# Twelve instead of six Strassen blocks in the first matrix, C11 begun by a bank-to-bank copy, score products as single blocks, sums added by transfers

## The chip, the cores and the metric

One core of a Trainium2 chip runs the whole program. The metric is the device time of one execution in microseconds, the median of the runs; lower is better. The engines are TensorE (PE; its weight loads are listed apart as PEld), VectorE (DVE), ScalarE (ACT), GpSimd (POOL) and SyncE (SP). POOL and SP issue nearly all transfers; each engine takes its instructions strictly in the order of its own program.

## The reference

Sparse attention is followed by a two-layer network, with batch 4, 8 heads, 768 positions and head size 64. A query sees the first 8 positions and the last 96, with a linear bias by distance.

```python
scores = scale * np.matmul(q, k.transpose(0, 1, 3, 2))
...
scores = np.where(keep, scores + bias, -1e9)
a = softmax(scores)
x = (a @ v) as 3072 tokens x 512
h = x @ w_in            # 512 x 2048, the first matrix
g = h - np.tanh(h)
out = g @ w_out         # 2048 x 512, the second matrix
```

## The kernel before

**Tiles.** The 3072 tokens are 24 units u of 128 queries, the four batches' first units ahead of all others. A unit has one or two blocks of keys (its own, o=0, and the one before it, o=1). For a unit the steps are: loads lq, lk, lv; transposes T (on PE with copies Te for the first seven units, by DMA on SP later); score products S (L396); the exponential E on ScalarE (L403); the mask M on VectorE; the product with v, AV (L427), whose 65th column is the sum of a row; its reciprocal R; the normalised x, N (L444); a transpose into xT (X and Xe on PE for eight units, Xe by DMA on SP later).

**First matrix.** The units are taken in groups: 0 and 1 alone, 2 to 11 in pairs (groups 2 to 6), and then fours (group 7 is units 12 to 15, 8 is 16 to 19, 9 is 20 to 23). A plain step m1 (L477) multiplies weights with xT into one PSUM bank; th takes tanh on ScalarE (L576) and g subtracts on VectorE (L590), into the tile gall. For groups of four, a block j of four 128-wide column blocks can be done by the Winograd form of Strassen's method instead: seven products d1 to d7 of half the size (L536, 28 matmuls of 256 columns where the plain way has 16 of 512). In before six blocks are done so (DUNITS): j = 1 to 3 of groups 8 and 9. Their sums of inputs are y (of x) and v (of weights). Copies e0, e1 and e2 keep the partial results of bank r; VectorE adds them back: q11 (L547), q21 and q22 (L550). tanh and g (L562, L568) then take 1024 columns at a time.

**Second matrix.** All twelve pairs of units are done in this form: p1 to p7 (L645, eight matmuls each), input sums n1 to n4 on VectorE (L630), weight sums w1 to w4 once, copies a0 to a2 out of bank r into the tile sn, and results c11, c21, c22 (an add on VectorE, L659) and c12 (a copy). Stores st go out from POOL or SP (L662). Where p6 adds onto bank r, it waits until a0 has read p1 there.

**Order.** No scheduler decides on the chip: the string ORDER lists every step in one sequence, each engine's program is the steps that fall to it in that order, and a suffix /a, /d, /p or /s picks ScalarE, VectorE, POOL or SP. HOMES gives each step its buffer or its PSUM banks (eight banks of 512 floats, which all these steps share). The score products of units 8 and up are written three blocks at a time, 24 matmuls in a row (the list runs, step S.n); those of units 0 to 7 are written unit by unit. So PE has 19 runs of score products.

## Time and profile before

| what | value |
|---|---|
| median of 3 runs | 201.99 us (201.69 to 202.01) |
| span of the profiled execution | 199.8 us |
| PE busy | 193.1 us, 97% of the span |
| VectorE busy | 178.6 us, 89% |
| ScalarE busy | 135.1 us, 68% |
| POOL busy | 75.3 us, 38% |
| chain that ended last, PE's share | 85% |

The profile gives the span from the first to the last instruction of one execution; its own run time is not given beside it, and the span lies 2.2 us under the runs' median. Matmuls are pipelined: a row's duration runs from issue to modelled end and overlaps with the next, so the price of a product on PE is the distance from its start to the start of the next. In a row of the timeline the columns are start, duration, engine, line, operation, written<-read, shape and count; idle time ahead of it stands in brackets with what ended it. A row of the groups gives, after the count, the busy time, the mean in ns of one, and idle time with what ended it.

### The profile page before, as it was taken

The page shows a single profiled execution, that of the slowest core. Times are in us where ns is not written, and L with a number is a line of the kernel's source. Part 1 is how long each engine was busy: PE and PEld are TensorE (multiplying, and loading weights), DVE is VectorE, ACT ScalarE, POOL GpSimd, SP SyncE. Part 2 cuts the span into 40 slices and gives each one's busy share as a digit, 9 for nine tenths or more (in the row PEclk, how much of TensorE's full clock was granted, in tenths as well). Part 3 has the DMA queues.
Part 4 walks back from the last instruction along what each step waited for, and adds up shares of the span by engine and source line. Part 5 has one row for each costly group of instructions (what it writes and reads, how often), then busy time and mean ns, then how long its engine had stood idle before and what let it go on. Part 6 is the DMA issues. An engine that isn't in the chain of part 4 may idle for free.

```text
span 199.8 us, 5524 instructions
## 1 busy us (share of the span) xinstructions
PE 193.1 (97%) x2219; PEld 157.8 (79%) x2219; DVE 178.6 (89%) x348; ACT 135.1 (68%) x234; POOL 75.3 (38%) x97
## 2 busy tenths in 40 slices
PE   8799999999999999999999999999999999999992
PEld 2469998888888988988898655688898687888892
DVE  6487599999999999999999898999999999999942
ACT  3698898726569559758947789578778777464220
POOL 8987576350694057069207904702000100001110
PEclk9999999999999999999999999999999999999999
DMA  5999999999999999989996998994733101001233
GB/s 148 211 180 185 198 163 207 201 156 141 193 167 196 178 153 135 133 188 171 137 158 146 140 173 192 154 155 85 55 108 121 66 0 54 3 0 52 107 132 131
DMA packets 103545, 27.36 MB, mean 137 GB/s; under 512 B 93920, under 2 KB 101472, under 8 KB 103520
## 3 DMA queue, kind: packets, MB, share of 16 engines
q0 software_dynamic: 74048, 16.78, 89.5%
q1 hardware_dynamic: 28928, 9.70, 27.6%
q10 hardware_dynamic: 544, 0.52, 1.0%
q8 instruction: 17, 0.28, 0.5%
q14 instruction: 8, 0.07, 0.1%
HBM read 27.26 MB, written 6.29 MB: 168 GB/s over the span
## 4 chain that ended last, share of the span: by engine, by line
PE 85%; DVE 7%; DMA 3%; ACT 2%; issue 1%; ACTq 0%; DVEq 0%
PE ps L645 36%; PE ps L477 27%; PE ps L536 9%; PE ps L396 5%; PE ps L427 5%; DMA f<-in_q_dram 3%; DVE gall L590 2%; DVE x L444 2%; DVE mem L407 1%; PE ps L455 1%; ACT mem L403 1%; PE ps L320 1%; ACT mem L274 1%; PE ps L365 1%; ACT th L576 1%
## 5 line engine op out<-in xcount | busy, mean ns | idle before, releaser
L477 PE MATMUL ps<-xT,w_in_bf 128*128 128x256 bf16 (+2 forms) x544 | 69.0, 279 | 0.0
L477 PEld LDWEIGHTS <-w_in_bf 128*128 128x128 bf16 x544 | 47.2, 98 | 12.4
L576 ACT ACTIVATE th<-ps 128x512 f32<-128x512 f32 (+1 forms) x74 | 41.8, 591 | 18.7 <-PE ps L477 13.6
L590 DVE TENSOR_TENSOR gall<-ps,th 128x512 bf16<-128x512 f32 (+1 forms) x74 | 47.4, 668 | 6.0 <-ACT th L576 5.6
L645 PEld LDWEIGHTS <-gall 128*128 128x128 bf16 x488 | 46.4, 98 | 7.0
L662 POOL DMA_DIRECT2D out_dram<-ot x14 | 8.1, 580 | 102.5 <-ACT ot L274 52.4
L403 ACT ACTIVATE mem<-ps 128x1024 bf16<-128x1024 f32 x44 | 43.3, 1024 | 4.3 <-PE ps L396 4.2
L645 PE MATMUL ps<-w_out_bf,gall 128*128 128x256 bf16 (+1 forms) x296 | 36.3, 270 | 0.0
L274 ACT COPY sn<-ps 128x256 f32<-128x256 f32 x32 | 12.0, 375 | 20.3 <-PE ps L645 16.3
L645 PE MATMUL ps<-f,ss 128*128 128x256 bf16 x192 | 24.9, 273 | 0.0
L645 PE MATMUL ps<-wc,gall 128*128 128x256 bf16 x192 | 24.9, 273 | 0.0
L342 POOL DMA_DIRECT2D vb<-in_v_dram x24 | 21.5, 900 | 2.2 <-issue 1.0
L645 PEld LDWEIGHTS <-ss 128*128 128x128 bf16 x192 | 18.3, 98 | 2.8
L342 POOL DMA_DIRECT2D mem<-in_k_dram x20 | 17.9, 899 | 4.8 <-DMA w_out_bf<-in_moe_w_out_dram 3.1
L342 POOL DMA_DIRECT2D mem<-in_q_dram x20 | 18.1, 904 | 3.8 <-DMA w_out_bf<-in_moe_w_out_dram 3.0
L412 DVE TENSOR_TENSOR mem<-mem,mk 128x2048 bf16<-128x2048 bf16 x16 | 19.2, 1215 | 0.0
L659 DVE TENSOR_TENSOR ot<-ps,sn 128x256 f32<-128x256 f32 x36 | 14.7, 415 | 3.6 <-ACT sn L274 2.5
L444 DVE TENSOR_TENSOR x<-ps,rden 128x512 bf16<-128x512 f32 x23 | 15.8, 687 | 0.5
L274 ACT COPY mem<-ps 128x512 f32<-128x512 f32 (+1 forms) x22 | 12.7, 585 | 5.1 <-PE ps L536 3.9
L427 PEld LDWEIGHTS <-mem 128*128 128x128 bf16 x352 | 13.4, 97 | 2.1 <-ACT mem L403 0.5
L427 PE MATMUL ps<-vb,mem 128*128 128x65 bf16 x352 | 14.7, 193 | 0.0
L396 PE MATMUL ps<-mem 64*128 64x128 bf16 x352 | 13.1, 217 | 0.0
(78 smaller groups left out, 220.7 us busy)
## 6 DMA issues: line engine op xcount, KB each, us to landing
out_dram<-ot POOLq DMA_DIRECT2D x14, 256.0 KB, 2.8
vb<-in_v_dram POOLq DMA_DIRECT2D x24, 128.0 KB, 6.2
mem<-in_q_dram POOLq DMA_DIRECT2D x22, 128.0 KB, 6.3
mem<-in_k_dram POOLq DMA_DIRECT2D x22, 128.0 KB, 6.1
out_dram<-ot SPq DMA_DIRECT2D x9, 256.0 KB, 2.0
w_out_bf<-in_moe_w_out_dram POOLq DMA_DIRECT2D x4, 512.0 KB, 10.7
w_in_bf<-in_moe_w_in_dram POOLq DMA_DIRECT2D x4, 256.0 KB, 7.6
w_in_bf<-in_moe_w_in_dram POOLq DMA_DIRECT2D x2, 512.0 KB, 11.0
```

Of the source, the lines that this page charges most:

```text
L274: nc.scalar.copy(out=out, in_=in_)
L342: eng(e).dma_start(out=dst, in_=rows_of(src, u).rearrange("h p d -> p h d"))
L396: nc.tensor.matmul(bank(("s", u, o), hh)[:, p * P : (p + 1) * P], buf(("qk", back[u] if o else u))[r, 1, p, :], buf(("qk", u))[r, 0, p, :] ...
L403: nc.scalar.activation(d, banks(("s", u, o), 0, 1), AF.Exp, bias=0.0, scale=scale)
L412: nc.vector.tensor_tensor(out=t, in0=t, in1=mk[:, 1:3], op=ALU.mult)
L427: nc.tensor.matmul(t[:, h // (H // 2), h % (H // 2), :], buf(("p", u, o))[:, slot(h), :], buf(("v", back[u] if o else u))[:, h, 0 : Dh + 1 ...
L444: nc.vector.tensor_tensor(out=buf(("x", u)).rearrange("q (a h) d -> q a h d", a=2), in0=t[:, :, :, 0:Dh], in1=rden.to_broadcast([P, 2, H / ...
L477: nc.tensor.matmul(t[:, (f - f0) * n : (f - f0 + 1) * n], w_in_bf[j][:, c, fo : fo + P], x[:, c, 0:n], start=(c == 0), stop=(c == CD - 1),)
L536: nc.tensor.matmul(t[:, r * 2 * P : (r + 1) * 2 * P], w(r)[:, c], x[:, c], start=first and r + c == 0, stop=c == 1, skip_group_check=not f ...
L576: nc.scalar.activation(h_view(buf(("th", g, f0)), g, m), h_view(bank(("h", g, f0)), g, m), AF.Tanh, bias=0.0, scale=1.0)
L590: nc.vector.tensor_tensor(out=o, in0=v(h), in1=v(th), op=ALU.subtract)
L645: nc.tensor.matmul(bank((holder, a))[:, c0:c1], s(f), t(f)[:, c0:c1], start=first and f == 0, stop=f == HF - 1, skip_group_check=not first,)
```

## The change

**More Strassen blocks.** DUNITS now holds j = 0 to 3 of groups 7, 8 and 9, twelve blocks. Of the plain steps of 512 columns none is left. The sums of the weights have a tile of their own (ws), and the shared buffers mem go from 23 to 20, xT from 4 to 3, ss from 5 to 3.

**C11 begun by a copy.** In both matrices, the copy of the first product (a0, e0) now goes from bank r to bank q, always on ScalarE, and the second product (p2, d2) adds onto it. The adds q11 are gone, and c11 is a plain copy, on ScalarE for eight pairs and on VectorE for four. p2 and d2 now wait for a0 and e0.

**Sums by transfer.** The signs of the weight sums are turned so that n3 and n4 are additions into gall; eleven of the 24 (n4 of pairs 8 to 16 and 20, n3 of pairs 10 to 14, 18 and 20) are issued from POOL as transfers that add onto their destination. gall is laid out unit by unit for that, and the products of a Strassen block write each bank in two pieces of 128 columns, 256 apart.

**Score products.** Each block of eight is a step of its own, S.u.o, and ORDER places them one by one. Neighbours on PE counted as one, there are 25 runs.

**Order.** ORDER and HOMES are new throughout. Stores: 15 on SP and 11 on POOL, against 12 and 14.

```diff
-m1.4.14 g.4.10 M.8 a1.4/a S.9 th.4.14 T.11 p5.4 g.4.14 E.9.1 V.7/d p2.4 a2.4/d E.10.0 M.9 T.12 m1.4.2 E.10.1 n4.4/d
...
+th.5.8 y1.7 m1.6.4 g.5.10 e0.7.0 lv.19 th.6.2 y2.7 c21.6 lk.22 d6.7.0 g.5.8 S.18.1 e1.7.0/a lv.18 v4.0 d2.7.0 th.6.4
...
+n2.22/d p3.18 n4.22/d p6.22 c12.18/a c21.16 st.18.0/s p4.18 a1.22/a n2.20/d p5.22 c21.18 n4.20/p st.19.0/s p6.20
...
-    NM, NV, NG, NSS, NSN = 23, 12, 5, 5, 4
+    QUADS = 12
+    NM, NV, NG, NSS, NSN, NXT = 20, 12, 5, 3, 4, 3
...
-    DUNITS = [(8, 1), (8, 2), (8, 3), (9, 1), (9, 2), (9, 3)]
+    DUNITS = [(g, j) for g in range(7, 10) for j in range(4)]
...
-    THREES = 8
...
-        else:
-            runs += [[(u, 0), (u, 1), (u + 1, 0)], [(u + 1, 1), (u + 2, 0), (u + 2, 1)]]
...
-    gall = pool.tile([P, NG, CF, 2 * P], BF16, name="gall")
+    gall = pool.tile([P, NG, 2, CF, P], BF16, name="gall")
...
-    def a_S(xs):
-        for u, o in xs:
-            for p in range(NP):
-                for hh in range(2):
-                    r = slice(hh * Dh, (hh + 1) * Dh)
-                    nc.tensor.matmul(
-                        bank(("s", u, o), hh)[:, p * P : (p + 1) * P], buf(("qk", back[u] if o else u))[r, 1, p, :],
-                        buf(("qk", u))[r, 0, p, :], start=u >= BIASED, stop=u >= BIASED or p == NP - 1,
-                    )
+    def a_S(u, o):
+        for p in range(NP):
+            for hh in range(2):
+                r = slice(hh * Dh, (hh + 1) * Dh)
+                nc.tensor.matmul(
+                    bank(("s", u, o), hh)[:, p * P : (p + 1) * P], buf(("qk", back[u] if o else u))[r, 1, p, :],
+                    buf(("qk", u))[r, 0, p, :], start=u >= BIASED and p == 0, stop=p == NP - 1,
+                )
 
...
     def d_keep(g, j, k):
-        return buf(("k0", g, j)) if k == 0 else mems(("k12", g, j), FP32)[:, (k - 1) * 4 * P : k * 4 * P]
+        return d_bank(g, j, "q") if k == 0 else mems(("k12", g, j), FP32)[:, (k - 1) * 4 * P : k * 4 * P]
...
-            2: ("q", lambda r: w_in_of(a + r, 2), x_block(g, 2, 1), True),
+            2: ("q", lambda r: w_in_of(a + r, 2), x_block(g, 2, 1), False),
...
-        t = d_bank(g, j, part)
+        t = d_bank(g, j, part).rearrange("q (t r n) -> q t r n", t=2, r=2)
...
-                    t[:, r * 2 * P : (r + 1) * 2 * P], w(r)[:, c], x[:, c], start=first and r + c == 0, stop=c == 1,
+                    t[:, :, r, :], w(r)[:, c], x[:, c], start=first and r + c == 0, stop=c == 1,
...
-        if k == 0:
-            q = d_bank(g, j, "q")
-            nc.vector.tensor_tensor(out=q, in0=q, in1=d_keep(g, j, 0), op=ALU.add)
-            return
...
-        o, x, y, op = {
-            1: (lambda: buf(("ss", a, 1)), lambda: a21, lambda: a22, ALU.add),
-            2: (lambda: buf(("ss", a, 2)), lambda: buf(("ss", a, 1)), lambda: a11, ALU.subtract),
-            3: (lambda: a21, lambda: a11, lambda: a21, ALU.subtract),
-            4: (lambda: a12, lambda: a12, lambda: buf(("ss", a, 2)), ALU.subtract),
-        }[k]
-        eng(e).tensor_tensor(out=o(), in0=x(), in1=y(), op=op)
+        (a11, a12), (a21, a22) = ((gall[:, i, t, 0:HF, :], gall[:, i, t, HF:CF, :]) for t in range(2))
+        one = lambda: buf(("ss", a, 1))
+        two = lambda: buf(("ss", a, 2))
+        o, x, y = {
+            1: lambda: (one(), a21, a22), 2: lambda: (two(), one(), a11),
+            3: lambda: (a21, a21, a11), 4: lambda: (a12, a12, two()),
+        }[k]()
+        if e is POOL:
+            nc.gpsimd.dma_start(out=o, in_=y, accum_op=ALU.add)
+        else:
+            eng(e).tensor_tensor(out=o, in0=x, in1=y, op=ALU.add)
...
-            2: ("q", lambda f: g_of(a, HF + f), w(1, 0), True),
+            2: ("q", lambda f: g_of(a, HF + f), w(1, 0), False),
...
     def keep(e, a, k):
-        copy(e, buf(("sn", a, k)), bank(("r", a))[:, 0:DH2])
+        copy(e, buf(("sn", a, k)) if k else bank(("q", a))[:, 0:DH2], bank(("r", a))[:, 0:DH2])
 
     def result(e, a, i, j, c0=0, c1=DH2):
         o = buf(("ot", a + i - 1))[:, (j - 1) * DH2 + c0 : (j - 1) * DH2 + c1]
-        if (i, j) == (1, 2):
-            copy(e, o, bank(("r", a))[:, c0:c1])
+        if i == 1:
+            copy(e, o, bank(("qr"[j - 1], a))[:, c0:c1])
             return
-        holder, k = {(1, 1): ("q", 0), (2, 1): ("z", 1), (2, 2): ("z", 2)}[i, j]
-        nc.vector.tensor_tensor(out=o, in0=bank((holder, a))[:, 0:DH2], in1=buf(("sn", a, k)), op=ALU.add)
+        nc.vector.tensor_tensor(out=o, in0=bank(("z", a))[:, 0:DH2], in1=buf(("sn", a, j)), op=ALU.subtract)
...
-            op((f"e{k}", g, j), None, lambda e, g=g, j=j, k=k: d_copy(e, g, j, k))
-        for w, k in (("q11", 0), ("q21", 1), ("q22", 2)):
+            op((f"e{k}", g, j), None if k else ACT, lambda e, g=g, j=j, k=k: d_copy(e, g, j, k))
+        for w, k in (("q21", 1), ("q22", 2)):
...
-            op((f"a{k}", a), None, lambda e, a=a, k=k: keep(e, a, k))
+            op((f"a{k}", a), None if k else ACT, lambda e, a=a, k=k: keep(e, a, k))
...
-            op((f"c{i}{j}", a), None if (i, j) == (1, 2) else DVE, lambda e, a=a, i=i, j=j: result(e, a, i, j))
+            op((f"c{i}{j}", a), None if i == 1 else DVE, lambda e, a=a, i=i, j=j: result(e, a, i, j))
```

The program of ScalarE in the last third, before: three copies of bank r (the last is e2 of block 1 of group 9), a0 of pair 16 into sn, tanh of a plain step, a copy e2, tanh of a Strassen block, a1.

```order
L274 COPY mem_81<-ps_61 128x512 x3
L274 COPY sn0_108<-ps_61 128x256
L576 ACTIVATE th_101<-ps_61 128x512
L274 COPY mem_81<-ps_61 128x512
L562 ACTIVATE th_101<-ps_61 128x1024
L274 COPY sn3_111<-ps_61 128x256
```

The same engine and place after: e0 of block 3 of group 9, e2 of block 1, a0 of pair 16, a tanh, c11 of pair 16 (ps is PSUM, mem, sn and ot are SBUF).

```order
L267 COPY ps_61<-ps_61 128x512
L267 COPY mem_81<-ps_61 128x512
L267 COPY ps_61<-ps_61 128x256
L551 ACTIVATE th_101<-ps_61 128x1024
L267 COPY ot2_113<-ps_61 128x256
```

The copies e0 and a0 now write PSUM, the plain tanh of 512 columns is gone, and c11 has come to this engine as a copy.

The program of POOL around the last loads, before: two stores, the loads of k 23, v 18 and v 20, a store, and v 22.

```order
L662 DMA out_0_dram<-ot1_114 128x512
L662 DMA out_0_dram<-ot3_116 128x512
L342 DMA mem_81<-in_k_dram 128x8x64
L342 DMA vb2_84<-in_v_dram 128x8x64
L342 DMA vb5_87<-in_v_dram 128x8x64
L662 DMA out_0_dram<-ot0_113 128x512
L342 DMA vb4_86<-in_v_dram 128x8x64
```

After: v 18, k 20, a store, the first transfer that adds (n4 of pair 8), then the loads of q 21, v 23 and v 20 and a store.

```order
L335 DMA vb6_88<-in_v_dram 128x8x64
L335 DMA mem_81<-in_k_dram 128x8x64
L657 DMA out_0_dram<-ot2_113 128x512
L624 DMA gall_102<-ss1_104 128x1024
L335 DMA mem_81<-in_q_dram 128x8x64
L335 DMA vb1_83<-in_v_dram 128x8x64
L335 DMA vb2_84<-in_v_dram 128x8x64
L657 DMA out_0_dram<-ot0_111 128x512
```

The transfer into gall stands among the loads: POOL waits there for n2 and p2 of pair 8, and the loads behind it wait along.

More of the change, by code (lines that the diff above doesn't have):

```diff
@@ L478, in m1 @@
                     t[:, (f - f0) * n : (f - f0 + 1) * n], w_in_bf[j][:, c, fo : fo + P], x[:, c, 0:n],
-                    start=(c == 0), stop=(c == CD - 1),
+                    start=f == f0 and c == 0, stop=(c == CD - 1),
+                    skip_group_check=f > f0,
                 )
@@ L494, in wsum @@
     def wsum(j, k):
[L495 removed]
+        return ws[:, j, k - 1]
     def xsum(g, k):
@@ L734 @@
             op(("Xe", u), SP, lambda e, u=u: a_DX(u))
-    for n, xs in enumerate(runs):
-        op(("S", n), PE, lambda e, xs=xs: a_S(xs))
+    for u in range(NU):
+        for o in blocks_of(u):
+            op(("S", u, o), PE, lambda e, u=u, o=o: a_S(u, o))
     for g, us in enumerate(groups):
```

242 lines of the change are left out of this document (119 added, 123 removed).

## Prediction

> **What bounds the kernel now.** I read the page first: busy time, slices, the chain that ended last.
>
> ```profile
> span 199.8 us, 5524 instructions
> PE 193.1 (97%) x2219; PEld 157.8 (79%) x2219; DVE 178.6 (89%) x348; ACT 135.1 (68%) x234; POOL 75.3 (38%) x97
> PE   8799999999999999999999999999999999999992
> DVE  6487599999999999999999898999999999999942
> PE 85%; DVE 7%; DMA 3%; ACT 2%; issue 1%; ACTq 0%; DVEq 0%
> ```
>
> TensorE is busy 97% of the span and carries 85% of the chain. A busy share alone does not prove a bound, so next come the waits of PE, then its busy time by stage.
>
> ```profile
> PE ps L361 <- ACT mem L274: 1.2, 1, 1.2
> PE ps L795 <- DVE vb L316: 1.0, 1, 1.0
> PE ps L455 <- DVE x L444: 0.9, 3, 0.4
> 58.00:130.00 72.00, 72.00 (x855) 57.31 (x854) 67.97 (x126) 53.20 (x96) 34.67 (x43) 1.00 1.61 161
> 130.00:180.00 50.00, 50.00 (x510) 41.32 (x508) 49.93 (x86) 37.21 (x62) 2.04 (x3) 1.00 0.36 64
> ```
>
> In these two windows (columns: PE, PEld, DVE, ACT, POOL, clock) PE is busy for every one of 122 us at a granted clock of 1.00. The first two waits belong to the start, which the change leaves as it is; the last, 0.9 us, is all that PE still loses to another engine. So the time after the start is the sum of PE's products, and the change is worth what it does to that sum, plus whatever new waits it makes. VectorE is the second limit: 49.93 of 50 us busy from 130 to 180, yet without holding PE up.
>
> **The products of the first matrix.** The timeline gives starts; the distance between starts is a product's price, since ends overlap.
>
> ```profile
> 118.84 3.62 PE L477 MATMUL ps<-xT,w_in_bf 128*128 128x512 bf16 x16
> 122.29 0.65 PE L427 MATMUL ps<-vb,mem 128*128 128x65 bf16 x16
> 143.57 1.04 PE L536 MATMUL ps<-mem 128*128 128x256 bf16 x8
> 144.45 1.04 PE L536 MATMUL ps<-xT,w_in_bf 128*128 128x256 bf16 x8
> 145.32 0.60 PE L536 MATMUL ps<-xT,mem 128*128 128x256 bf16 x4
> ```
>
> Sixteen 512-wide matmuls take 122.29 - 118.84 = 3.45 us. That is one block (four columns of blocks, 512 tokens) done plainly. Sixteen 256-wide ones take 145.32 - 143.57 = 1.75 us, 0.109 each, so a Strassen block of 28 costs 3.06. Saved: 0.39 us a block. Six more blocks (group 7's four, block 0 of groups 8 and 9): -2.3 us. Nothing hides this, PE being full.
>
> **The score products.** They contract over 64 rows; all around them contracts over 128.
>
> ```profile
> 51.27 1.04 PE L645 MATMUL ps<-w_out_bf,gall 128*128 128x256 bf16 x8
> 52.24 0.62 PE L396 MATMUL ps<-mem 64*128 64x128 bf16 x16
> 52.79 0.66 PE L427 MATMUL ps<-vb,mem 128*128 128x65 bf16 x16
> 61.58 1.04 PE L477 MATMUL ps<-xT,w_in_bf 128*128 128x256 bf16 x8
> 62.55 0.84 PE L396 MATMUL ps<-mem 64*128 64x128 bf16 x24
> 63.32 1.05 PE L645 MATMUL ps<-f,ss 128*128 128x256 bf16 x8
> 64.21 1.04 PE L645 MATMUL ps<-w_out_bf,gall 128*128 128x256 bf16 x8
> ```
>
> Sixteen score matmuls take 0.55 us from start to start, 24 take 0.77: 0.22 for a block of eight. The run of 24 should then be 0.66, and is 0.11 longer. The eight wide matmuls ahead of it should take 0.87 and take 62.55 - 61.58 = 0.97, 0.10 more; those behind it take 0.89. Each run of score products so costs about 0.23 us beyond its matmuls, whatever its length. In the table of before, 44 blocks stand in 19 runs; in that of after, counting neighbours on PE as one, in 25 (four single ones for the first batch rows as before, then pairs, two runs of three, and four lone blocks: S.16.1, S.18.1, S.19.0, S.21.0). Six more runs: +1.4 us. So the smaller pieces give back over half of what Strassen saves.
>
> **VectorE, ScalarE and the copies.** Rows of the groups:
>
> ```profile
> L590 DVE TENSOR_TENSOR gall<-ps,th 128x512 bf16<-128x512 f32 x70 | 45.8, 682 | 5.5 <-ACT th L576 5.2
> L568 DVE TENSOR_TENSOR gall<-ps,th 128x1024 bf16<-128x1024 f32 x6 | 7.3, 1219 | 0.0
> L550 DVE TENSOR_TENSOR mem<-ps,mem 128x512 f32<-128x512 f32 x12 | 8.2, 682 | 0.0
> L547 DVE TENSOR_TENSOR ps<-ps,mem 128x512 f32<-128x512 f32 x6 | 4.1, 687 | 0.0
> L659 DVE TENSOR_TENSOR ot<-ps,sn 128x256 f32<-128x256 f32 x36 | 14.7, 415 | 3.6 <-ACT sn L274 2.5 <-PE ps L645 0.8
> L630 DVE TENSOR_TENSOR gall<-gall 128x1024 bf16<-128x1024 bf16 x12 | 8.2, 681 | 0.0
> L509 DVE TENSOR_TENSOR mem<-w_in_bf 128x512 bf16<-128x512 bf16 x5 | 2.1, 413 | 0.0
> L576 ACT ACTIVATE th<-ps 128x512 f32<-128x512 f32 x70 | 40.2, 602 | 18.7 <-PE ps L477 13.6 <-DVE rden L433 1.9 <-DVE gall L590 1.3
> L562 ACT ACTIVATE th<-ps 128x1024 f32<-128x1024 f32 x6 | 6.2, 1037 | 0.3 <-PE ps L536 0.2
> L274 ACT COPY sn<-ps 128x256 f32<-128x256 f32 x32 | 12.0, 375 | 20.3 <-PE ps L645 16.3
> L274 ACT COPY mem<-ps 128x512 f32<-128x512 f32 x18 | 10.3, 585 | 4.1 <-PE ps L536 3.9
> ```
>
> VectorE loses six adds of line 547 (4.1), eleven sums of line 630 that become transfers (7.5), 24 narrow subtractions (16.4) and eight net of the 0.415 us ops on C11 (3.3): -31.3. It gains 12 wide subtractions (14.6), 12 adds of line 550 (8.2), eight sums of inputs (3.3) and about 2 us of copies: +28. Net -3 us, from 178.6 to about 175. ScalarE loses 24 narrow tanh (14.4) and gains 12 wide ones (12.4), 17 copies of 512 (9.9) and seven net copies of 256 (2.6): +10, to 145, 73% of the span. Neither becomes the bound by its sum, and PE's sum does not see them.
>
> The bank-to-bank copy is now ahead of a product: p2 adds onto what a0 wrote, d2 onto e0. For a block of the first matrix d6, which adds onto the bank that e0 reads, already waited for that copy, and after has d2 behind d6 or no nearer to e0. No row shows a copy into PSUM; the nearest are 375 and 585 ns into SBUF, which I take. Between p1 and p2 PE has at least 0.87 us of other products, so the term is zero if ScalarE is free, and the second rival if not.
>
> **The rest.** The eleven accumulating transfers are new; the first rival prices them, and I take zero. They stand on POOL, where n4.8 holds back loads of q 21 and v 23 and 20 until p2.8 has been; those keep 5.9 us and more of PE work ahead of their use. With 20 buffers instead of 23 the tightest load, v 10, keeps 6.0 us between its place and its product, where before the tightest kept 7.9. Stores move from POOL to SP (12 to 15 there), ahead of transposes whose shortest cover is 3.9 us.
>
> ```profile
> L662 POOL DMA_DIRECT2D out_dram<-ot x14: 542/582/645, 51.3 to 192.2; - x14
> DMA to landing us min/median/max: 1.7/2.3/5.8
> L342 POOL DMA_DIRECT2D vb<-in_v_dram x24: 876/895/962, 4.4 to 138.5; - x24
> DMA to landing us min/median/max: 3.6/6.2/13.7
> 195.60 0.61 PE L645 MATMUL ps<-w_out_bf,gall 128*128 128x128 bf16 x8
> 195.80 0.42 DVE L659 TENSOR_TENSOR ot<-ps,sn 128x256 f32<-128x256 f32 x1 [0.58 <-PE ps L645]
> 196.24 0.29 DVE L276 COPY ot<-ps 128x128 f32<-128x128 f32 x1
> ```
>
> Each pair of rows is an issue line and the landing times of its transfers. A load takes 0.9 to issue and 6.2 to land, so v 10 may be late by up to a microsecond; slack in the score blocks ahead of it makes me take zero here, with +1 in the range. At the end, the last copy ran at 196.24, behind a VectorE op that waited for p4 of the last pair. After, p4.22 comes earlier and the last quarter is copied by ScalarE directly behind its product: a copy of 128 instead of two ops, -0.1 us.
>
> **Sum.** -2.3 + 1.4 - 0.1 = -1.0 us against the profiled span: 199.8 becomes 198.8. The runs' median, 201.99, lies 2.2 over that span, and I carry the 2.2 along: 201.0. About 0.2% (0.4 us) is what a measurement of this kernel can tell from no change.
>
> **Rival 1, slower: the accumulating transfers come late.** Between its place in the table and the product that needs it, n4.20 has five products of 0.87 on PE (p6.20, p7.22, p5.20, p4.22, p7.20, then p3.20), 4.4 us; n4.12 has 4.9, n4.8 5.1, n4.14 5.2, the other seven 7.0 and more. A store of the same 256 KB takes 0.58 to issue and 1.7 to 5.8 to land: 2.9 us at the median, 6.4 at most. If the sum needs both operands read, twice the median landing gives 5.2: n4.20 is 0.8 late, n4.12 0.3, n4.8 0.1, and these 1.2 us use up the gain (202.2). At 5.8 the stalls are 1.4 + 0.9 + 0.7 + 0.6 = 3.6, so 204.6; at 6.4 they are 2.0 + 1.5 + 1.3 + 1.2 = 6.0, so 207.0. It decides from 5.1 us on. For it: no transfer in this trace adds. Against it: late in the run the queues are nearly empty (DMA share 0.36 from 130 to 180). The Trainium skill (DMA: Bandwidth & Descriptors, anatomy of one DMA) fits 2.0 us plus bytes over 436 GB/s to a transfer of this path, which would make 2.6 here and no stall at all. Chance 13%; its time 204.6.
>
> **Rival 2, no change: products wait behind the copies.** Where one ScalarE op stands between the product and its copy, the copy ends late if that op has only just begun: p1.10 (a 1.04 tanh and 0.375 against 0.88 of cover, 0.5), p1.4 (exp, 0.3), d1.7.0 (0.3), d1.8.2 (0.3), p1.0, p1.16, d1.7.3 (0.1 each). All at their worst make 1.7 us, 202.7; half, 201.9. For it: ScalarE rises to 73%. Against it: before has the same cover of 0.87 in front of p6 and d6, and no wait of PE for such a copy. Chance 20%.
>
> **Rival 3, much slower: scattered outputs.** The 336 products of Strassen blocks now write two pieces of 128 into their bank instead of 256 in a row. No row shows such an output. If one cost 10% more (11 ns), 336 would cost 3.7 us and make 204.7; 3 ns would use up the gain. The Trainium skill states that rule: any non-contiguous access pattern slows matmuls significantly (PSUM — Partial Sum Buffer, specifications); no run here shows it. The pieces are 512 bytes long, so I give it 3%.
>
> **Rival 4, faster still.** VectorE's 3 us less also take PE's 0.9 us of waits for x away: 200.1. Against it: those waits lie before 58 us, where the load of VectorE hardly falls. Chance 13%.
>
> **How the numbers follow.** My sum gets 48%, with 200.4 to 201.6 as its own range; the rivals 13, 20, 3 and 13; 3% are for what I don't see. The range 200.0 to 203.7 leaves out the larger part of rival 1, rival 3, the lower end of rival 4 and most of the rest, together 2 in 10. Faster: nearly all of my sum, rival 4 and a little of rival 2, 0.61. Same: the middle of rival 2, 0.14. Slower: rivals 1 and 3 and the rest, 0.25.
>
> **What would show it.** Right: no 512-wide first-matrix matmul left after group 6; 28 matmuls of a block still in 3.06 us; 25 runs of score products with 0.23 around each; PE's own waits still under 1 us after the start. Wrong: PE waits on the transfer into gall ahead of p7 or p3 near the end (rival 1), on ps copied by ScalarE ahead of p2 or d2 (rival 2), or distances over 0.109 between products of a block (rival 3).

## The result

The changed kernel is 1.6% slower: the ratio to the kernel before is 1.016 (95% interval 1.013 to 1.019), about 205.0 us against 201.8. The forecast was 201.0, and the range ended at 203.7. Some executions of a kernel take longer, here three of six (208.6 to 212.7 us, against 203.9 to 205.8); times and ratios leave them out, but the traces of y3, w2, q4 and a2 show one, so the lengths of their waits prove nothing alone. The profiled execution, the shortest of the six, took 203.88 us with a span of 202.1, 2.3 us over the span before. That the mean lies another 1.1 us higher, no trace of this kernel shows in detail; the control w0 below, which differs only in the buffers of activated pairs, has further waits behind 90 us.

The page of the changed kernel, the same lines as before:

```profile
span 202.1 us, 5665 instructions
PE 191.2 (95%) x2291; PEld 163.7 (81%) x2291; DVE 176.0 (87%) x335; ACT 144.3 (71%) x244; POOL 83.0 (41%) x105
PE   7699998999999986899999999999999999999992
PE 74%; DMA 15%; ACT 3%; SPq 2%; issue 1%; DVE 1%; POOL 1%; ACTq 0%; POOLq 0%; DVEq 0%
```

PE has 1.9 us less to do, and the span is longer. The chain that ended last now runs over transfers for 15% (3% before), and PE's slices (of 5 us each) fall to 8, 6 and 8 from 71 to 86 us. The same place in two windows, of the kernel before and then of the changed one (us, busy of PE, PEld, DVE, ACT, POOL, clock, DMA share, GB/s; the DMA share adds up several queues and so can exceed 1):

```profile
70.00:85.00 15.00, 15.00 (x206) 13.15 (x205) 14.26 (x28) 11.22 (x19) 6.71 (x8) 1.00 1.66 139
```

```profile
70.00:85.00 15.00, 11.91 (x181) 9.53 (x179) 12.25 (x26) 10.55 (x18) 7.87 (x9) 1.00 1.93 179
```

PE loses 3.1 us of busy time in these 15 us, while transfers move more (179 GB/s against 139). What it waits for there, from the timeline of the changed kernel:

```profile
73.14 0.66 PE L419 MATMUL ps<-vb,mem 128*128 128x65 bf16 x16 [0.23 <-DMA vb<-in_v_dram]
...
76.53 1.03 PE L641 MATMUL ps<-wc,gall 128*128 128x256 bf16 x8 [1.20 <-DVE ot L654]
...
78.45 0.40 PE L388 MATMUL ps<-mem 64*128 64x128 bf16 x8 [0.34 <-DVE x L436]
79.47 1.91 PE L469 MATMUL ps<-xT,w_in_bf 128*128 128x256 bf16 x16 [0.62 <-DMA xT<-x]
...
84.31 0.84 PE L388 MATMUL ps<-mem 64*128 64x128 bf16 x24 [0.70 <-DMA mem<-mem]
```

In turn: v of unit 10; the product p4.4, whose bank VectorE empties late (by c22.4); the x of unit 10, which VectorE works out behind c22.4; the transposed x of units 8 and 9; the transposed unit 13. By distances from start to start, with each matmul at its usual price, PE loses 4.3 us from 70 to 90 us against 0.45 before: about 0.4, 1.4, 0.5, 0.8 and 0.9 at these five places, and the rest around score products. Summed so over the whole run: matmuls -2.6, the first 70 us -0.3, 70 to 90 us +3.8, later (mostly the six more runs of score products) +1.3. That makes +2.2 of the 2.3 us measured.

The queues behind these waits, from the timelines of VectorE, POOL and SP in the changed kernel:

```profile
76.05 0.42 DVE L654 TENSOR_TENSOR ot<-ps,sn 128x256 f32<-128x256 f32 x1 [1.94 <-DMA out_dram<-ot]
...
56.62 0.89 POOL L335 DMA_DIRECT2D mem<-in_k_dram  x1 [10.31 <-DVE mem L399]
...
74.09 0.87 POOL L335 DMA_DIRECT2D vb<-in_v_dram  x1 [5.02 <-PE ps L419]
...
55.87 13.65 SPq L370 DMA_TRANSPOSE mem<-mem  x3
69.58 0.97 SPq L657 DMA_DIRECT2D out_dram<-ot  x1
...
76.54 1.47 SPq L370 DMA_TRANSPOSE mem<-mem  x1
```

POOL stands for 10.3 us with the load of k 15, whose buffer is still in use, and all later loads stand behind it; then ten go out 0.87 us apart. SP therefore gets the transposes of 12 and 15 only after 66 us, the store of rows 0 behind them at 69.6, and c22.4, which needs that store's buffer, waits until 76. So the 1.4 and 0.5 us at p4.4 and the x of unit 10 hang on a store that lands late. At 74 us POOL has stood for another 5.0 us, with the load of v 13. The last row is the transpose of unit 13. Transfers issued at 77 us land late (last column, us):

```profile
vb<-in_v_dram POOLq DMA_DIRECT2D x1, 128.0 KB, 7.8
mem<-mem SPq DMA_TRANSPOSE x1, 7.7
```

76.54 + 7.73 = 84.27, and the scores of unit 13 start at 84.31. In the kernel before, the same unit's transpose, issued at 68.56, took 4.8.

**Lead.** I matched each transfer by its place in its queue with the step on PE that reads it, and took its lead: from landing to first use. Times in us:

| unit | scores at, before | lead | scores at, after | lead |
|---|---|---|---|---|
| 12 | 73.6 | 4.2 | 73.7 | 2.6 |
| 13 | 78.2 | 4.9 | 84.3 | 0.05 |
| 14 | 89.5 | 2.9 | 77.5 | 0.6 |
| 15 | 89.9 | 4.2 | 78.5 | 3.3 |
| 17 | 106.7 | 2.6 | 95.7 | 0.05 |
| 18 | 107.1 | 3.8 | 97.9 | 4.4 |
| 19 | 112.6 | 2.6 | 112.8 | 0.05 |

The order needs units 14, 15, 17 and 18 from 9 to 12 us earlier, since group 7 as a Strassen group wants all of units 12 to 15 at once. That this is what brings 17 and 18, of group 8, forward as well was not looked into. For v, the shortest lead of units 8 to 23 was 2.3; now v 10 has 0.05 (11.3 before) and v 16 has 1.3.

### The profile page after: what moved, and what is told of

It is laid out like the page before. It is cut to its first block, busy times and chain, and to the rows that moved or that the text cites. A ratio compares the mean times of both kernels' runs of the same rounds, so it can differ in the third digit from the quotient of the medians.

```text
span 202.1 us, 5665 instructions
## 1 busy us (share of the span) xinstructions
PE 191.2 (95%) x2291; PEld 163.7 (81%) x2291; DVE 176.0 (87%) x335; ACT 144.3 (71%) x244; POOL 83.0 (41%) x105
## 4 chain that ended last, share of the span: by engine, by line
PE 74%; DMA 15%; ACT 3%; SPq 2%; issue 1%; DVE 1%; POOL 1%; ACTq 0%; POOLq 0%; DVEq 0%
PE ps L641 33%; PE ps L529 17%; PE ps L469 13%; DMA mem<-mem 7%; DMA mem<-in_q_dram 5%; PE ps L388 5%; PE ps L419 5%; DMA mem<-in_k_dram 3%; SPq L458 1%; ACT th L566 1%; POOL mem L332 1%; ACT mem L395 1%; DVE x L436 1%; ACT x L432 1%; PE ps L447 0%
## 5 line engine op out<-in xcount | busy, mean ns | idle before, releaser
L469 PE MATMUL ps<-xT,w_in_bf 128*128 128x256 bf16 (+1 forms) x448 | 46.7, 257 | 0.7 <-DMA xT<-x 0.6
L469 PEld LDWEIGHTS <-w_in_bf 128*128 128x128 bf16 x448 | 37.9, 98 | 4.7 <-issue 0.8
L581 DVE TENSOR_TENSOR gall<-ps,th 128x512 bf16<-128x512 f32 (+1 forms) x50 | 31.7, 662 | 3.8 <-ACT th L566 3.7
L566 ACT ACTIVATE th<-ps 128x512 f32<-128x512 f32 (+1 forms) x50 | 28.5, 589 | 8.2 <-PE ps L469 6.9
L335 POOL DMA_DIRECT2D mem<-in_k_dram x20 | 18.2, 911 | 12.5 <-DVE mem L399 10.3
L529 PE MATMUL ps<-mem,ws 128*128 128x256 bf16 x144 | 20.2, 273 | 0.0
L529 PEld LDWEIGHTS <-ws 128*128 128x128 bf16 x192 | 17.9, 98 | 2.4
L267 ACT COPY mem<-ps 128x512 f32<-128x512 f32 (+1 forms) x27 | 15.5, 586 | 5.2 <-PE ps L529 3.8
L624 POOL DMA_DIRECT2D gall<-gall x5 | 4.4, 878 | 32.6 <-DVE ss L626 32.6
L539 DVE TENSOR_TENSOR mem<-ps,mem 128x512 f32<-128x512 f32 x24 | 15.9, 682 | 0.8 <-PE ps L529 0.7
L267 ACT COPY ot<-ps 128x256 f32<-128x256 f32 (+1 forms) x20 | 7.2, 366 | 12.5 <-PE ps L641 12.4
```

The lines of the kernel that those rows point to most:

```text
L267: nc.scalar.copy(out=out, in_=in_)
L335: eng(e).dma_start(out=dst, in_=rows_of(src, u).rearrange("h p d -> p h d"))
L469: nc.tensor.matmul(t[:, (f - f0) * n : (f - f0 + 1) * n], w_in_bf[j][:, c, fo : fo + P], x[:, c, 0:n], start=f == f0 and c == 0, stop=(c = ...
L529: nc.tensor.matmul(t[:, :, r, :], w(r)[:, c], x[:, c], start=first and r + c == 0, stop=c == 1, skip_group_check=not first or r > 0,)
L539: nc.vector.tensor_tensor(out=a, in0=d_bank(g, j, "z"), in1=a, op=ALU.add)
L566: nc.scalar.activation(h_view(buf(("th", g, f0)), g, m), h_view(bank(("h", g, f0)), g, m), AF.Tanh, bias=0.0, scale=1.0)
```

## The experiments

Theories: A, the place of a transfer in SP's queue; B, want of buffers; C, the sums by transfer (in the run y4 it means the order on PE); D, transfers in flight slow each other; E, lead; F, engines other than the transfers. Moves in ORDER are shown as the words that moved.

**First set: A, B and C.** Two stores ahead of the transposes; a buffer of its own for k and q 15; both; and all n3, n4 back on VectorE.

```diff
 # x1_stores_early
-N.8/a st.0.0/s ... E.11.0 st.2.0/s
+c12.0/a st.0.0/s ... c12.2/d st.2.0/s
 # x2_buffer: far becomes a view of ws; x3_both: the two together
-NM, NV, NG, NSS, NSN, NXT = 20, 12, 5, 3, 4, 3
+NM, NV, NG, NSS, NSN, NXT = 21, 12, 5, 3, 4, 3
-kq.15:6
+kq.15:20
 # x4_sums_dve
-n4.8/p ... n4.20/p   (eleven words)
+n4.8/d ... n4.20/d
```

> The changed kernel with two stores moved up in the order, still on SP: st.0.0 right behind c12.0 (ahead of T.9) and st.2.0 right behind c12.2 (ahead of T.12). Theory A (stores stand behind transposes on SP and hold the output buffers): the 1.9 us that VectorE waited for a store's end ahead of c22 of pair 4 goes, with it PE's 1.4 us ahead of p4.4, and T.13 comes 0.6 us earlier; PE loses 1 to 1.5 us between 70 and 85 us instead of 4, the span falls from 202.1 to 199.5 to 200.5. Theory B (the loads come late because buffers are missing, and everything behind them): the stores only waited because T.12 and T.15 did; PE still loses 2.5 us or more there, at S.13 and the groups' first products, and the span stays over 201. Theory C (the sums by transfer): no change.

Measured: 212.4 us, ratio 1.055 (1.051 to 1.059). The waits grew to 10.6 us between 70 and 90 us; the longest:

```profile
84.97 3.44 PE L469 MATMUL ps<-xT,w_in_bf 128*128 128x256 bf16 x16 [3.84 <-DMA xT<-x]
```

The loads issued from 56 to 66 us beside the earlier stores landed in 7.9 us (median for k) instead of 5.2. A's cure fails: ahead of the transposes, the stores cost more than behind them.

> The changed kernel with one more buffer of mem (21) that q and k of unit 15 have for themselves; the tile far, used at the start alone, becomes a view of ws to make room. Theory B: the load of k 15 no longer waits 10 us on POOL, and v 9 behind it neither; those two go out at 46 to 48 us; q 12, which waits for AV.7 in its own buffer, at about 57 us. The burst behind it starts with two loads fewer, so T.12 and T.15 come about 1.7 us earlier and PE loses 1.5 to 2 us less: span about 200.3. Theory A: the stores keep their place behind T.15, so what T.15 gains they gain, up to 1 us. Theory C: no change.

Measured: 207.4 us, 1.029 (1.026 to 1.032); the span is 206.1, not B's 200.3. POOL stood as long, now with the next load in line (q 12, 10.0 us); the waits of 74 to 85 us stayed, and one of 2.1 us on the transposed unit 17 came at 98 us.

> Both edits together: two stores up in SP's order and a buffer of its own for q and k of unit 15. If A and B are both causes, PE loses under 1 us between 70 and 85 us, the span is 198.5 to 199.5 and the runs lie 0.2 to 0.7% under the kernel before; if only one is, the span is that of its own run within 0.3 us.

Measured: 206.8 us, 1.029 (1.022 to 1.035); waits of 1.8 us on v 10, 1.1 on x, 1.3 on unit 17.

> The changed kernel with all 24 sums n3 and n4 on VectorE, none by transfer. Theory C (the transfers that add hold POOL's loads or fill the queues): the span falls below 201 and the runs lie closer together. Theories A and B: the stalls between 70 and 85 us come before the first such transfer (113 us) and stay; VectorE gets 11 x 0.68 = 7.5 us more behind 100 us, where it is 92 to 96% busy, so the span stays within 0.5 us or grows by up to 3.

Measured: 210.8 us, 1.047 (1.045 to 1.049). The span grows by 6.9 us, more than the 3 allowed for. Here VectorE makes PE wait late (0.7 us at 134, 0.5 at 157 among others), and most of the waits of 70 to 85 us stay (3.3 us of 4.3). The sums by transfer are worth having; C falls, and neither A nor B alone explains the loss.

**Second set: D against A.** y1 leaves out the loads of q and k of units 16 to 18; y2 moves the transpose of 13 forward and the store of rows 0 to ScalarE; y3 leaves the first three stores out.

```diff
 # y1_no_burst, in load_natural
+        if src is not v and u in (16, 17, 18):
+            return
 # y2_sp_order
-T.14 Xe.8 Xe.9 st.2.0/s T.13 ... N.8/a st.0.0/s
+T.14 T.13 Xe.8 Xe.9 st.2.0/s ... c12.4/a st.0.0/a
 # y3_no_stores, in store
+        if u < 3:
+            return
```

> The changed kernel without the six loads of q and k of units 16, 17 and 18 (0.79 MB; their scores are worked out from what the buffers held before, so the output of these units is wrong). They belong to the burst of nine loads that GpSimd issues between 74 and 82 us, beside which transposes and stores land in 7.7 us. Theory D (transfers that are in flight together slow each other, and the transposes of units 12 to 15 have too little lead for that): loads, the transposes of x and the transpose of unit 13 land in 4 to 5 us again, the waits of TensorE on them between 78 and 85 us (0.6 and 0.7 us, with 0.8 beside them) go, and the time falls by 1.5 to 2.5 us, to 201.5 to 202.5. Theory A (a transpose comes late because of its place in SyncE's queue, whatever else is in flight): the transposes are issued at the same times, the waits stay, and the time stays at 203.9 or more.

Measured: 204.3 us, 1.012 (1.010 to 1.015), close to the changed kernel and not D's 201.5 to 202.5. As D has it, the transpose of unit 13 lands in 6.1 us instead of 7.7 and PE no longer waits for it, and the next two, of x of 11 and 10, land in 2.4 us each instead of 6.1 and 5.3. But p4.4 still waits (1.27), and so does the product on x of 8 and 9:

```profile
79.75 1.91 PE L471 MATMUL ps<-xT,w_in_bf 128*128 128x256 bf16 x16 [1.11 <-DVE mem L406]
```

The row names a mask on VectorE, which ended at 79.65 us behind the same late c22.4, but the transposed x of 9 landed only at 79.61 (79.34 in the changed kernel): issued ahead of the loads left out, it is no faster. Smaller waits follow at 101 and 119 us.

> The changed kernel with two steps moved on the queues: the transpose of unit 13 is issued right behind that of unit 14 (ahead of the transposes of x of units 8 and 9 and of the store of rows 2), and the store of rows 0 is issued by ScalarE behind c12.4, at about 64 us, in place of SyncE's 69.6 us. All bytes stay. Theory A (order on SyncE): the wait of 0.87 us on the transpose of unit 13 at 84 us and the wait of 1.38 us on the output buffer at 76 us go, the transposes of x come 1.4 us later and cost 0 to 0.7 us more: 201.5 to 202.5. Theory D (transfers in flight together): what is issued earlier lands beside the ten loads of 57 to 65 us and slows them; the waits move to other transfers, and the time stays between 203 and 207, as with the stores moved ahead (212.4).

Measured: 211.8 us, 1.050 (1.046 to 1.053). Unit 13 then has 11 us of lead; v 10 comes 1.9 us late, and x of units 8 and 9, behind it on SP, 4.9 us. A falls as a cure.

> The changed kernel without the stores of rows 0, 1 and 2 (0.75 MB of output are not written). SyncE has three steps fewer between 55 and 77 us, and c22.4 finds its output buffer free. Theory A: T.12 is issued no earlier (it waits for its load), but the wait of 1.38 us at 76 us goes and T.13 is issued 0.6 to 1.5 us earlier: 1.5 to 2.3 us less, 201.6 to 202.4. Theory D: the same wait goes, and beside it the loads and transposes land 0.5 to 1 us sooner, so that the waits on v 10, x of 8 and 9 and unit 13 (0.4, 0.8, 0.87) shrink too: 2.5 to 4 us less, 200 to 201.4. If neither the stores' bytes nor their place matter, 203.9 stays.

Measured: 204.5 us (205.1 and 203.8), 1.014 (1.009 to 1.018), as the changed kernel, where A and D both had forecast 200 to 202.4. In the traced execution (207.0 us) p4.4 no longer waits, AV of unit 13 comes at 87.2 instead of 89.6 us, and the win is given back ten microseconds later:

```profile
77.90 1.91 PE L469 MATMUL ps<-xT,w_in_bf 128*128 128x256 bf16 x16 [1.32 <-DVE ss L626]
93.89 0.40 PE L388 MATMUL ps<-mem 64*128 64x128 bf16 x8 [0.74 <-DVE x L436]
96.38 0.40 PE L388 MATMUL ps<-mem 64*128 64x128 bf16 x8 [2.09 <-DMA mem<-mem]
```

The last row waits for the transposed unit 17. It is issued at 91.4 us in the changed kernel and at 90.8 here, and takes 5.5 us instead of 4.2, so it lands at 96.3 instead of 95.6: that PE has come 2.4 us further does not bring it forward.

A further run moved the scores of units 13 and 15 behind two products.

```diff
 # y4_scores_later
-S.13.1 ... S.13.0 ... S.15.1 ... m1.5.2 ... m1.5.4
+m1.5.2 ... m1.5.4 S.13.1 S.13.0 S.15.1
```

> The changed kernel with the scores of unit 13 and the second block of unit 15 (and their exponentials) moved on TensorE (and ScalarE) behind the next two first-matrix products of group 5, m1.5.2 and m1.5.4, about 1.8 us. No transfer is touched. Theory C (lead: the transfers are as they are, and the order asks for what they bring too early; other products stand ready): the wait of 0.87 us at 84 us goes, nothing comes late in its place, 203.0. Theories A and D both allow this as well, but where what follows (AV.13 to AV.15, x of 12 to 15) has no slack either, the wait turns up there: 203.5 to 204.5.

Measured: 207.6 us, 1.029 (1.025 to 1.032). The scores there overwrite the bank of m1.5.4 ahead of its second reader, so this is not the same computation; PE waited 2.9 us for exponentials in place of 0.7 for the transpose. It tells little.

**Third set: lead and the price of earlier loads.** Four buffers for activated pairs in place of five free 8 KB a partition (w0, the control). w1 spends it on buffers for loads, w2 also moves the transpose of 13. z1 and b1 put twelve idle matmuls into the changed kernel and the kernel before.

```diff
 # w0_ng4
-NM, NV, NG, NSS, NSN, NXT = 20, 12, 5, 3, 4, 3
+NM, NV, NG, NSS, NSN, NXT = 20, 12, 4, 3, 4, 3
-g.12:3 g.14:4 g.16:0 g.18:1 g.20:2 g.22:3
+g.12:0 g.14:3 g.16:1 g.18:2 g.20:0 g.22:3
 # w1_buffers: NM 22, NV 15 as well
-kq.15:6 kq.12:12 v.10:1 v.13:10 v.12:4
+kq.15:20 kq.12:21 v.10:12 v.13:13 v.12:14
 # w2_buffers_t13: w1 and
-T.14 Xe.8 Xe.9 st.2.0/s T.13
+T.14 T.13 Xe.8 Xe.9 st.2.0/s
 # z1_idle (b1_before_idle: zero:4 ahead of S.10)
-S.11.0
+zero:0 zero:0 ... zero:0 S.11.0   (twelve)
```

> A control: the changed kernel with four buffers for the activated pairs in place of five (the pairs 12 to 22 get other numbers), which frees 8 KB a partition and uses it for nothing. If no product waits for a pair's buffer, it runs as the changed kernel does, 203.9 to 206; a wait for a buffer would show on VectorE's first writes of groups 7, 8 or 9 and add that much.

Measured: 206.2 us, 1.017 (1.006 to 1.028), as the changed kernel. Its trace (206.3 us) has the same waits from 70 to 85 us, except on unit 13, and then 1.3 us on the transposed unit 17 at 97 and 0.8 on an x at 136.

> As the control, with the freed space made into two more buffers for q and k and three more for v (loads k and q of unit 15 and 12, v of 10, 12 and 13 get buffers of their own; no step is moved in any queue). Theory E (lead: GpSimd's loads stand still from 46 to 57 us and from 65 to 74 us because their buffers are still read, so the transposes and v of units 10 to 19 land with no lead, 0.05 to 0.7 us against 2.3 us or more in the kernel before): the ten loads that began at 56.6 us begin at 47 to 50 us, the store of rows 0 behind the transposes of 12 and 15 comes before 66 us, the waits between 70 and 85 us (4.3 us) fall under 1.5 us, and the time is 200.5 to 202. Rival F (the loads were not what held it: VectorE, exponentials and the order on SyncE come next): the loads come earlier, the waits are named after something else, and the time stays above 203.

Measured: 211.9 us, 1.050 (1.042 to 1.058): E's forecast failed outright. The loads did start earlier (46 to 54 us), and the transposes of units 8 to 11, which in the changed kernel move at that time with few loads beside them, took 2.6 times as long to land. Issues of 46 to 60 us, the changed kernel and then w1, and PE in w1:

```profile
mem<-mem SPq DMA_TRANSPOSE x4, 3.5
```

```profile
mem<-mem SPq DMA_TRANSPOSE x4, 9.2
```

```profile
59.11 0.62 PE L388 MATMUL ps<-mem 64*128 64x128 bf16 x16 [1.60 <-DMA mem<-mem]
59.66 1.05 PE L641 MATMUL ps<-f,ss 128*128 128x256 bf16 x8
65.51 1.03 PE L388 MATMUL ps<-mem 64*128 64x128 bf16 x16 [4.80 <-DMA mem<-mem]
```

So loads issued by POOL slow transposes issued by SP, as D has it. The Trainium skill (DMA: Bandwidth & Descriptors, Issuing engines are not separate DMA queues) says that what the engines issue ends up on the same sixteen transfer engines and interleaves there. These rows agree: 3.5 becomes 9.2 us.

> As the one with more buffers, and the transpose of unit 13 issued right behind that of unit 14, ahead of the transposes of x of 8 and 9 and the store of rows 2. Theory E: also the wait of 0.87 us on unit 13 at 84 us goes; 199.8 to 201.5, at or under the kernel before. Rival F: as the run without it or slower (alone, with the store of rows 0 moved too, this step gave 211.8).

Measured: 209.3 us, 1.036 (1.027 to 1.046); the same wait (4.8 us) at 66 us, and unit 13 gives none.

> The changed kernel with twelve idle matmuls of zeros (512 columns, about 0.216 us each, 2.6 us) put on TensorE right ahead of the scores of unit 11, at 70.4 us, where the waits begin. If the transfers lack lead once (they run on their own and are late by a few us): the idle matmuls lie where TensorE would have waited, the 4.3 us of waits between 70 and 85 us fall by 2 to 2.6, and the time is that of the changed kernel within 0.7 us, 203.5 to 206. If the loads are released by what TensorE itself gets done (buffers freed by scores and AV), the delay is handed on to them: the waits stay and the time is 2.6 us longer, 206.5 or more.

Measured: 207.2 us, 1.025 (1.018 to 1.033). Rows of its timeline:

```profile
71.08 2.75 PE L792 MATMUL ps<-zero 128*128 128x512 bf16 x12
...
83.92 0.84 PE L389 MATMUL ps<-mem 64*128 64x128 bf16 x24
```

PE does nothing useful for 2.7 us and reaches the scores of unit 13 at 83.9 us, against 84.3 without the idle work; the waits of 70 to 90 us fall from 4.3 to 0.7. Up to here the transfers set the time and PE had to stand anyway. Beyond that the time fits the second branch (206.5 or more): part of the delay is handed on. The load of v 13, released by PE's progress, goes out at 77.0 us instead of 74.1; with it the following loads move back, the transpose of 13 lands in 4.6 us instead of 7.7, and those of 16 and 17 come at 93.1 and 97.1 instead of 90.5 and 95.6. Later PE waits 1.1 us at 96, on an x, and 1.9 at 137, on a transpose; the whole is 1.0 us over the control beside it, with intervals that overlap.

> The kernel before, with the same twelve idle matmuls (2.6 us) put ahead of its run of scores at 73 us, a control for the run with idle matmuls in the changed kernel, where they cost nothing up to 90 us. The kernel before has no wait of TensorE there and 2.3 us or more of lead on every transfer: if TensorE is its bound, all 2.6 us are added, 204.2 to 204.6. If the kernel before also waits for transfers somewhere later, part of it comes back: under 203.5.

Measured: 204.4 us, 1.014 (1.012 to 1.016): all 2.7 us are added, and no wait goes. The kernel before is bound by PE at the same place.

**Fourth set: bytes moved or added.** q1 gives rows 0 to 2 output buffers of their own and stores them at about 139 us. q2 and q4 add moves.

```diff
 # q1_quiet_stores: w0 and
-    buffers("ot", 4, [P, DM], FP32)
+    buffers("ot", 7, [P, DM], FP32)
-ot.0:0 ot.1:1 ot.2:3
+ot.0:4 ot.1:5 ot.2:6
+Xe.20 st.1.0/s st.0.0/s st.2.0/s   (moved here)
 # q2_all: q1 and  v.10:12, T.14 T.13, T.17 T.18, lk.19 lq.19, Te.6.0/d n2.0/d
 # q4_lead: ot 6, NM 21, qk.17:20, v.10:12; st.0.0 and st.2.0 behind Xe.20,
 #   lk.16 lk.17 ahead of lk.18, T.17 ahead of T.18, lk.19 lq.19, Te.6.0/d n2.0/d
```

> As the control with four buffers for activated pairs, the freed space made into three more output buffers (rows 0, 1 and 2 get their own), and the stores of rows 0, 1 and 2 moved from 55 to 77 us to behind the transpose of x of unit 20, at about 139 us, where few transfers are in flight. The whole output is written. Theory D (one queue of transfers in effect, some 0.9 us for each 128 KB, which is full from 57 to 90 us): the three stores were worth six loads, c22.4 finds its buffer free, and the waits between 70 and 90 us (about 4 us) fall to about 1.5, as in the run without these stores; but the transpose of unit 17 still lands at about 96 us, and TensorE waits there for what it had won: 203 to 205. If the wait at 76 us and the stores were the whole cause: 200.5 to 202.

Measured: 205.2 us (206.7 and 203.7), no interval. In the traced one, of 206.7 us, p4.4 does not wait, as D expected, and the time is lost on x of 9 and on unit 17:

```profile
78.84 1.91 PE L469 MATMUL ps<-xT,w_in_bf 128*128 128x256 bf16 x16 [1.49 <-DMA xT<-x]
...
96.71 0.55 PE L388 MATMUL ps<-mem 64*128 64x128 bf16 x8 [1.51 <-DMA mem<-mem]
```

> As the run with quiet stores, and four steps moved to where the traces showed no lead: the transpose of unit 13 behind that of 14, that of unit 17 ahead of that of 18 and of the transpose of x of 12, the load of q 19 behind that of k 19, the sum n2.0 on VectorE behind the copy of unit 6; and v 10 gets a buffer of its own, so that its load needs no wait. Theory D with the lead restored: waits between 70 and 120 us under 1.5 us in all, the products of the two matrices as in the changed kernel: 199 to 201, at or under the kernel before (201.5 to 201.8). If something other than the transfers of 55 to 110 us costs the changed kernel its time, it stays over 203.

Measured: 214.8 us, 1.064 (1.056 to 1.072). The transpose of unit 17 there overwrites exponentials that AV of 14 still has to read, so part of the output is another. Unit 13 ahead of x on SP again costs: 5.9 us of wait on x.

> The changed kernel with four buffers for activated pairs, two more output buffers, one more for q and k (the transposed unit 17, which so far had to wait for AV of 14) and one more for v (v 10). The stores of rows 0 and 2 go behind the transpose of x of unit 20; the transpose of unit 17 goes ahead of that of 18 and of x of 12, the loads of k 16 and 17 ahead of k 18, the load of q 19 behind k 19, the sum n2.0 behind the copy of unit 6. Unit 13 stays where it was. Theory D with lead (transfers of 57 to 105 us are what costs): v 10, the output buffer, unit 17 and unit 19 give no wait any more, the wait on x of 9 at 78 us (about 1.5 us) stays: 200.5 to 203. If the waits only move to the next transfers: 204 or more.

Measured: 208.4 us (207.0 and 209.9), 1.034 (1.025 to 1.043): the waits only move, as the other branch (204 or more) has it. In the traced execution (213.4 us) v 10, the output buffer, unit 17 and unit 19 give no wait, as expected, and others do:

```profile
79.61 3.39 PE L470 MATMUL ps<-xT,w_in_bf 128*128 128x256 bf16 x16 [2.72 <-DMA xT<-x]
98.66 0.62 PE L389 MATMUL ps<-mem 64*128 64x128 bf16 x16 [2.31 <-DVE x L437]
```

Last, the stores of rows 0 to 2 issued twice in each kernel, the copies into rows that are written again later.

```diff
 # b2_before_double, a2_double, in store
+        if u < 3:
+            far_u = turn_of[u + 20] * P
+            eng(e).dma_start(out=out[far_u : far_u + P, c0:c1], in_=buf(("ot", u))[:, c0:c1])
```

> The kernel before with each store of rows 0, 1 and 2 issued twice, the second time into rows that later stores write again: 0.75 MB more between 51 and 72 us, with the work of the engines unchanged. If the kernel before lives on lead (2.3 us and more between the landing of a transfer and its use), it takes this in: 201.6 to 202.6, no wait of TensorE over 0.5 us between 70 and 120 us. If it is as near to the limit of the transfers as the changed kernel is, it loses 2 us or more: 203.6 and up.

Measured: 204.2 us, 1.009 (1.005 to 1.013). I had expected the kernel before to take this in (201.6 to 202.6). Two executions do, at 202.4 us; six take 204.0 to 204.8. The traced one, of 204.2 us, has one wait and none behind it:

```profile
79.16 1.03 PE L477 MATMUL ps<-xT,w_in_bf 128*128 128x256 bf16 x8 [2.04 <-DMA xT<-x]
```

In the kernel before, x of unit 8 lands at 75.5 us and is used at 77.0: 1.5 us of lead, less than the 2.3 that I had named for "every transfer", which holds for v and the transposed units from 8 up. So the kernel before is itself within 2 us of the limit of its transfers there.

> The changed kernel with the same doubling (rows 0, 1 and 2 stored twice, at 55, 70 and 76 us). It has no lead left there, so what these stores take from the transfers in flight is waited for: 1.5 us or more beyond the changed kernel, 206.5 to 210, with the waits again on transposes of units 12 to 17 and of x, 8 and 9. If transfers were not what holds it, it stays at 204 to 206.

Measured: 206.3 us, one execution to be compared, so no interval: 0.5 us over the longest of the changed kernel's three, and just short of the 206.5 from which the forecast held. In the traced one (211.6 us) PE waits 2.5 us on a transpose at 77 us, as expected, and 2.9 at 85 behind a mask.

The same 0.75 MB costs the kernel before 1.9 us; what it costs the changed kernel stays open.

**What follows.** Shown: in the changed kernel the transfers of 70 to 90 us set the time there, since PE can do 2.7 us of idle work without coming later to unit 13, while the kernel before pays for it in full (z1 against b1); loads brought forward delay the transposes (w1), and stores brought forward delay the loads (x1); more bytes there cost the kernel before (b2). Seen in single traces: with fewer bytes some waits there go (unit 13 in y1, p4.4 in y3 and q1), and others take up the win (unit 17 in y3 and q1). Argued, not shown: that bringing units 12 to 18 forward for the Strassen group is what used the lead up; no order with twelve blocks and the old lead was built, and no run that eased the transfers came out clearly under the changed kernel. No run reached the forecast of 201, and none beat the kernel before.

## Why the prediction was wrong

**The products (-2.3 us): right.** No 512-wide step is left. Timeline of the changed kernel:

```profile
117.14 0.60 PE L529 MATMUL ps<-xT,w_in_bf 128*128 128x256 bf16 x4
117.57 0.60 PE L529 MATMUL ps<-mem,w_in_bf 128*128 128x256 bf16 x4
...
126.90 0.40 PE L388 MATMUL ps<-mem 64*128 64x128 bf16 x8
127.23 0.61 PE L529 MATMUL ps<-mem,ws 128*128 128x256 bf16 x4
```

Four matmuls take 0.43 us, 0.108 each, so a block of 28 takes the 3.06 forecast. With it rival 3 falls: the outputs in two pieces cost nothing, and the rule of the Trainium skill (PSUM — Partial Sum Buffer, specifications) on scattered patterns does not show for pieces of 128 floats.

**The score products (+1.4): right.** There are 25 runs; one of eight takes 0.33 from start to start, 0.11 over its 0.22, and the eight wide matmuls ahead of a run take 0.10 more, as forecast.

**VectorE, ScalarE, the copies: right.** VectorE 176.0 (forecast 175), ScalarE 144.3 (145). The copies from bank to bank:

```profile
L267 ACT COPY ps<-ps 128x512 f32<-128x512 f32 x12 | 6.8, 575 | 0.6 <-PE ps L529 0.6
L267 ACT COPY ps<-ps 128x256 f32<-128x256 f32 x12 | 4.4, 371 | 1.6 <-PE ps L641 1.2 <-DVE gall L557 0.4
```

575 and 371 ns against 585 and 375 assumed, and among PE's waits none is on such a copy: rival 2 falls. PE's waits for an x come to 0.8 us against 0.9, so rival 4 brought nothing.

**The accumulating transfers: right at zero.** Rows of their landing:

```profile
gall<-ss POOLq DMA_DIRECT2D x6, 256.0 KB, 4.2
gall<-gall POOLq DMA_DIRECT2D x5, 256.0 KB, 3.3
```

The medians stay under the 5.1 from which rival 1 decides, and PE waits for none. It was a near thing: the longest took 6.0 us, but it was n3 of pair 10, with 7.0 and more of cover, while n4 of pair 12 took 4.8 of its 4.9. The fit cited beside it gave 2.6; the measured 3.3 to 4.2 decide.

**The tail (-0.1): right.** From the start of the last copies to the end, 3.5 us against 3.6.

**"The rest": this step failed.** It said that v 10 "keeps 6.0 us between its place and its product", that transposes have a "shortest cover" of 3.9 us, and took zero with +1 in the range. The stretch of 70 to 90 us cost 3.8 us. For v 10 the count was nearly true: its load went out 5.8 us ahead of its product, landed in 5.8 and cost 0.4. What failed was the zero for all the others: a store that kept an output buffer (1.9 us at p4.4 and the x behind it), for which the term had no price, the transpose of unit 13 (0.9) and the transposed x of 8 and 9 (0.8). Two errors in it. First, I counted PE's work between places in the order, as if a transfer were issued where it stands; POOL stood still for 10.3 and for 5.0 us, and SP behind its loads, so the issue comes when the whole line has moved. Second, I took landing times as fixed (6.2 for a load), where they depend on what else is in flight: the transpose of a unit lands in 3.1 to 8.0 us in this kernel, and the row that I had shown for loads ran from 3.6 to 13.7. I also looked at the stores moved late in the run, and passed over the three early ones between the transposes on SP. The sign came from there: without this term the sum was right to about 0.5 us for the profiled execution.

PE's 97% in the kernel before was true (b1) and misled: it says that transfers are in time, not by how much.

## What to carry to other kernels

Before pricing a new order, list for each transfer its lead, landing to first use, in the profile of before, and ask what the new order does to the smallest; a share of 97% hides leads of 1.5 and of 11 us alike. Where transfers are in flight without a pause, a load issued earlier can be another transfer's delay (w1), so that an order that needs data earlier has to find the room for it. Idle work put into both kernels at one place tells in two runs which of them is bound by the engine there: it cost the one 2.7 us and the other nothing up to that wait, though something later, because loads that the engine's progress releases had moved back.

## What the runs showed of the hardware

A long wait of PE costs twice. Windows of w1, around its wait of 4.8 us (us, busy of PE, PEld, DVE, ACT, POOL, granted clock, DMA share, GB/s), and two rows behind it:

```profile
60.00:64.00 4.00, 0.71 (x7) 0.39 (x4) 0.76 (x2) 1.48 (x2) 1.27 (x2) 0.86 1.76 150
64.00:68.00 4.00, 2.49 (x26) 1.99 (x27) 0.88 (x3) 1.79 (x2) 3.10 (x4) 0.50 1.65 195
68.00:72.00 4.00, 4.00 (x42) 3.10 (x41) 3.60 (x6) 2.70 (x5) 0.88 (x1) 0.78 2.41 161
```

```profile
66.87 1.92 PE L641 MATMUL ps<-w_out_bf,gall 128*128 128x256 bf16 x8
68.72 1.03 PE L388 MATMUL ps<-mem 64*128 64x128 bf16 x16
```

The granted clock falls to 0.50, and eight matmuls that take 0.87 us take 1.85. The waits of 1.2 us in the profiled changed kernel leave it at 1.00. The Trainium skill (TensorE: Matmul & The Clock Gate, What's actually happening) has the clock halved after a window of about 3.4 us without work. Here it fell sooner: a mean of 0.86 from 60 to 64 us makes 1.1 us at 0.50, so a drop at about 62.9 us (an estimate), 2.2 us after PE's last product had ended at 60.7. A shortage of transfers so makes itself worse. By the mean clock on record, 0.983 over the 209.9 us of this execution, about 7 us ran at half clock, which cost some 3.5 us of PE's work (an estimate too): part of why the variants lie 10 us apart.
